# Performer attention into a top-1 mixture of experts on one core: the batch-crossing chunk on the whole PE array, and the last expert slots in another order

## The chip, the cores and the metric

The kernel runs on one core of a Trainium2 chip. The metric is the time of one execution in microseconds of device time, the median of several runs. The engines are named as the profile names them: PE (TensorE; PEld is its weight load), DVE (VectorE), ACT (ScalarE), POOL (GpSimd) and SP (SyncE, which here only issues DMAs).

## The reference

```python
# attention: B=8, H=8, S=576, D=64, m=128 features
def phi(x):
    h = einsum('bhsd,md->bhsm', x, omega) - sum(x * x, -1, keepdims=True) / 2
    return exp(h - max(h, -1, keepdims=True)) / sqrt(m)
q_p, k_p = phi(q * scale), phi(k * scale)
kv = einsum('bhsm,bhsd->bhmd', k_p, v)
z = sum(k_p, axis=2)
num = einsum('bhsm,bhmd->bhsd', q_p, kv)
den = einsum('bhsm,bhm->bhs', q_p, z)[..., None] + 1e-06
x = (num / den).transpose(0, 2, 1, 3).reshape(4608, 512)
# mixture of experts: N=4608 tokens, D=512, 8 experts, F=1024
e_idx = argmax(x @ w_gate, 1)
for e in range(8):
    mask = e_idx == e
    h = maximum(x[mask] @ w1[e], 0)
    out[mask] = gate_w[mask, None] * sigmoid(x @ w_output_gate)[mask, e, None] * (h @ w2[e])
```

## The kernel before

**Units.** The attention is cut into 32 units `u`. A unit is one head in two batches, 2 x 576 tokens, which are 9 chunks of 128 tokens. Chunks 0 to 3 lie in the first batch, chunks 5 to 8 in the second, and chunk 4 has 64 tokens of either. Every float32 operand goes to PE as a float16 high half and a float16 low half, and a product is three matmuls: high by high, high by low, low by high. For each unit the step `pn` (in `attend`) multiplies the query features `et` (the weights that are loaded) by `kvs` (the moving operand: one column for the denominator, 64 of the numerator and 16 of the two gates, so 81 a batch). A chunk needs three matmuls. `pn` is cut in two at chunk 5, so that it fits a PSUM bank; the first part has chunks 0 to 4. Since `kvs` differs between the batches, chunk 4 is done twice in halves: its first 64 tokens against the first batch, its last 64 against the second, each with half of the PE array's columns (`128*64` in the profile). The step `xf` (in `divide`) then runs on DVE: add and scale the denominator, take its reciprocal, multiply. `xf` is what the gates and the experts work on.

**Slots.** The experts work on lists of tokens, 128 a list, called slots and numbered `n`. The lists of a group of units are made on the chip as soon as its gates are known; slots 0 to 24 belong to the first three groups, slots 25 to 48 to the last, and with this data slots 0 to 37 run. The steps of a slot are: `gx` (POOL gathers the token rows), `xt` (a transposing DMA on SP), `hA` and `hB` on PE (the two halves of the hidden layer, 48 matmuls each, written to PSUM tiles `ph`), `relu` on ACT (makes `hh`, the high half) and `rest` on DVE (makes `hl`, the low half) for each of the two, `out(n, 0)` and `out(n, 1)` on PE (the second layer into the PSUM tile `po`; in the last group `out(n, 0)` is joined to `hB`), `os` on ACT (scales into the buffer that is stored), and `put` (POOL stores the rows by an indirect DMA). A slot with at most 64 tokens takes a narrower form of these steps; slots 25, 26, 36 and 37 are of this kind.

**Weights.** An expert's weights come by DMA as float32 and are cut into four quarters of each layer. `swh` on ACT writes the high half of a quarter (`w1h`, `w2h`) and `swl` on DVE the low half (`w1l`, `w2l`). Both stand in the program of every slot, inside a branch that does the work only if the slot's expert differs from the last one. With this data that is so for slots 4, 12, 21, 26, 31 and 37. Slot 36 has no new expert, so its `swh` and `swl` are branches that do no work; PE still waits for them before it uses the weights.

**Order.** All steps stand in one list of 3318 numbers, `ORDER`, which is written out in the file, and every engine's queue has its own steps in that order. A second list, `BANKS`, says which PSUM bank each tile has. The end of the program is inside a branch that is taken only if more slots are needed (here it isn't). The puts of the last slots that can run (`LATE` of them, slots 34 to 37) are issued on POOL behind that branch and a drain of POOL's DMAs; their rows wait in the buffer `xt32`.

Of the kernel before, what the change touches and what calls it, by code (L numbers as in the profile page):

```python
# [10 lines left out]
F32 = mybir.dt.float32  # L11
# [4 lines left out]
ALU = mybir.AluOpType  # L16
# [5 lines left out]
P = 128  # L22
# [5 lines left out]
NC = 9  # L28
NCV = 10
NP = H // 2  # L30
# [35 lines left out]
LATE = 4  # L66
# [258 lines left out]
def attention_moe(ctx: ExitStack, tc: tile.TileContext, kqt, kqn, v, om, wg, w1, w2, cf, cm, ci, out):  # L325
# [162 lines left out]
    kvs = buf("kvs", 2, [2, W, 2], F16)  # L488
    kvf = buf("kvf", 2, [2, P], F16)
    xf = buf("xf", 2, [NC, D + GW], F32)  # L490
    den = buf("den", 2, [NC], F32)
    xs = buf("xs", 2, [NC, P], F32)
    lga = buf("lga", 2, [NC, GW], F32)

# [1279 lines left out]
```

## Time and profile before

| | us |
|---|---|
| median of 3 runs | 628.85 (627.51 to 632.21) |
| the profiled execution | 623.89 |
| its span | 622.0 |
| PE busy | 593.9 (95%) |
| ACT busy | 421.6 (68%) |
| DVE busy | 387.9 (62%) |
| POOL busy | 374.3 (60%) |

The span is the time from the first instruction to the last in the profiled execution; 1.89 us lie around it. An engine is busy while an instruction of it runs. Matmuls are pipelined, so their durations overlap: what a matmul costs PE is the time from its start to the next one's.

### The profile page before, as it was taken

The page shows a single profiled execution, that of the slowest core. Times are in us where ns is not written, and L with a number is a line of the kernel's source. Part 1 is how long each engine was busy: PE and PEld are TensorE (multiplying, and loading weights), DVE is VectorE, ACT ScalarE, POOL GpSimd, SP SyncE. Part 2 cuts the span into 40 slices and gives each one's busy share as a digit, 9 for nine tenths or more (in the row PEclk, how much of TensorE's full clock was granted, in tenths as well). Part 3 has the DMA queues.
Part 4 walks back from the last instruction along what each step waited for, and adds up shares of the span by engine and source line. Part 5 has one row for each costly group of instructions (what it writes and reads, how often), then busy time and mean ns, then how long its engine had stood idle before and what let it go on. Part 6 is the DMA issues. An engine that isn't in the chain of part 4 may idle for free. (4 is left out here: it accounts for less than half of the span.)

```text
span 622.0 us, 22247 instructions
## 1 busy us (share of the span) xinstructions
PE 593.9 (95%) x8716; PEld 471.6 (76%) x8716; DVE 387.9 (62%) x1219; ACT 421.6 (68%) x978; POOL 374.3 (60%) x275
## 2 busy tenths in 40 slices
PE   6999987999999899999999999999999999999995
PEld 6999876867786677778877777778867867677764
DVE  4777699866678987647797865543783530351124
ACT  6999999789889688989868787871522521351143
POOL 2265589789976688999788889985322111211203
PEclk9999997899999999999999999999999999999998
DMA  7655689999999999999989998778676647742671
GB/s 269 201 163 167 201 266 210 222 238 268 290 270 249 225 252 209 289 199 230 298 223 260 231 196 200 175 180 212 203 163 215 205 80 215 203 99 55 132 284 50
DMA packets 145888, 129.00 MB, mean 207 GB/s; under 512 B 104270, under 2 KB 127440, under 8 KB 144464
## 3 DMA queue, kind: packets, MB, share of 16 engines
q1 hardware_dynamic: 139760, 107.45, 69.1%
q0 software_dynamic: 5984, 19.72, 10.3%
q8 instruction: 80, 1.31, 0.9%
q14 instruction: 64, 0.52, 0.3%
HBM read 83.86 MB, written 19.30 MB: 166 GB/s over the span
## 5 line engine op out<-in xcount | busy, mean ns | idle before, releaser
L1586 PE MATMUL ph<-xt,w1h 128*128 128x128 f16 (+1 forms) x2432 | 206.8, 218 | 0.8 <-ACTq L1510 0.4
L1586 PE MATMUL ph<-xt,w1l 128*128 128x128 f16 (+1 forms) x1216 | 203.1, 218 | 0.4 <-DVEq L1515 0.4
L1586 PEld LDWEIGHTS <-w1h 128*128 128x128 f16 x2432 | 184.3, 98 | 9.0 <-issue 1.3
L623 ACT ACTIVATE ef<-pp,nb 128x128 f32<-128x128 f32 x576 | 163.0, 394 | 17.3 <-DVE nb L617 13.1
L604 DVE TENSOR_REDUCE pp<-pp 128x3 f32<-128x384 f32 x192 | 102.8, 557 | 33.2 <-PE pp L582 28.2
L1586 PEld LDWEIGHTS <-w1l 128*128 128x128 f16 x1216 | 118.5, 98 | 0.5 <-DVEq L1515 0.5
L646 POOL TENSOR_TENSOR es<-ef,es 128x1152 f16<-128x1152 f32 x44 | 104.5, 2385 | 20.1 <-ACT es L644 13.4
L1597 DVE SCALAR_TENSOR_TENSOR hl<-ph,hh 128x512 f16<-128x512 f32 (+1 forms) x76 | 50.4, 664 | 97.8 <-ACTq L1515 61.4
L1617 PE MATMUL po<-w2h,hl 128*128 128x512 f16 x280 | 106.1, 379 | 1.8 <-DVE hl L1597 1.8
L1617 PE MATMUL po<-w2h,hh 128*128 128x512 f16 x280 | 106.2, 379 | 0.2 <-PE ph L1586 0.2
L1617 PE MATMUL po<-w2l,hh 128*128 128x512 f16 x280 | 106.1, 379 | 0.0
L1549 POOL DMA_INDIRECT gx<-rows,gi x38 | 38.2, 1005 | 104.4 <-ACT os L1672 46.1
L1593 ACT ACTIVATE hh<-ph 128x512 f16<-128x512 f32 (+1 forms) x76 | 44.6, 590 | 83.0 <-PE ph L1586 69.3
L1617 PEld LDWEIGHTS <-hh 128*128 128x128 f16 x560 | 51.3, 98 | 52.7 <-issue 0.3
L516 POOL TENSOR_TENSOR xlo<-xt,xhi 128x1152 f16<-128x1152 f32 x24 | 57.2, 2383 | 10.8 <-ACT xhi L509 8.6
L1617 PEld LDWEIGHTS <-hl 128*128 128x128 f16 x280 | 27.4, 98 | 35.4 <-DVE hl L1597 2.5
L1672 ACT ACTIVATE os<-po,gx 128x512 f32<-128x512 f32 (+1 forms) x34 | 23.4, 687 | 43.8 <-PE po L1617 37.6
L644 ACT CAST es<-ef 128x1152 f16<-128x1152 f32 x44 | 51.5, 1181 | 0.7 <-ACTq L1510 0.2
L802 PE MATMUL pn<-kvs,et 128*128 128x81 f16 (+1 forms) x960 | 47.5, 204 | 0.9 <-ACT ef L623 0.5
L802 PEld LDWEIGHTS <-et 128*128 128x128 f16 (+1 forms) x960 | 40.5, 101 | 7.6 <-issue 0.5
L582 PE MATMUL pp<-omh,xhi 64*128 64x128 f16 x432 | 42.6, 223 | 2.9 <-ACT ef L623 1.9
L582 PE MATMUL pp<-omh,xlo 64*128 64x128 f16 x432 | 41.1, 222 | 0.7 <-POOL xlo L516 0.7
(193 smaller groups left out, 1059.6 us busy)
## 6 DMA issues: line engine op xcount, KB each, us to landing
r<-w SPq DMA_DIRECT2D x10, 2048.0 KB, 9.0
xt<-kqt SPq DMA_DIRECT2D x32, 576.0 KB, 5.3
xn<-kqn SPq DMA_DIRECT2D x24, 576.0 KB, 5.7
rawv<-v SPq DMA_DIRECT2D x32, 325.0 KB, 5.4
rows<-xs SPq DMA_DIRECT2D x16, 576.0 KB, 6.0
r<-w SPq DMA_DIRECT2D x8, 512.0 KB, 6.3
ef<-w SPq DMA_DIRECT2D x2, 512.0 KB, 3.9
et<-w SPq DMA_DIRECT2D x2, 512.0 KB, 8.0
```

The lines of the kernel that those rows point to most:

```text
L516: lambda t0=t0, t1=t1: nc.gpsimd.tensor_tensor(out=xl(u)[:, t0:t1], in0=xt32(u)[:, t0:t1], in1=xh(u)[:, t0:t1], op=ALU.subtract),
L582: nc.tensor.matmul(banks["pp", 2 * u + i, g][:, c, :], x[r, t], w[r, :], start=(a == 0), stop=(a == len(ops) - 1))
L604: nc.vector.tensor_reduce(out=pp[:, 3, 0:3], in_=pp[:, 0:3, :], op=ALU.min, axis=AX.X)
L623: nc.scalar.activation(ef(n)[:, c, :], banks["pp", n, g][:, c % 3, :], AF.Exp, bias=nb(n)[:, c : c + 1], scale=-SK)
L644: nc.scalar.copy(es(slot_es(n))[:, 0], ef(n))
L646: nc.gpsimd.tensor_tensor(out=es(slot_es(n))[:, 1], in0=ef(n), in1=es(slot_es(n))[:, 0], op=ALU.subtract)
L802: nc.tensor.matmul(pn[lo:hi, c - c0, :], a[:, c, lo:hi], w[:, :, b], start=(i == 0), stop=(i == len(ops) - 1))
L1549: nc.gpsimd.indirect_dma_start(out=gx(n), out_offset=None, in_=rows[0 : (j + 1) * NC * P], in_offset=bass.IndirectOffsetOnAxis(ap=tabs[gr] ...
L1586: nc.tensor.matmul(ph[:, f4, 0:w_], w[qd][:, kk, fo : fo + P], xt(n)[:, x, 0:w_], start=(a == 0), stop=(a == 3 * KC - 1))
L1593: nc.scalar.activation(hh(n)[:, sl, 0:w_], banks["ph", n, g][:, :, 0:w_], AF.Relu)
L1597: nc.vector.scalar_tensor_tensor(out=hl(n)[:, sl, 0:w_], in0=banks["ph", n, g][:, :, 0:w_], scalar=0.0, in1=hh(n)[:, sl, 0:w_], op0=ALU.ma ...
L1617: nc.tensor.matmul(po, x(n)[:, f, :], w[f // 2][:, f % 2, :], start=(f == 0 and a == 0), stop=(f == FC - 1 and a == 2))
```

## The change

There are three edits.

1. From unit 10 on, chunk 4 is multiplied on the whole array: each of its three matmuls has 128 weight columns (all tokens of the chunk) and 162 moving columns (`kvs` of both batches side by side). The result takes two rows of the PSUM tile, which is now 6 x 81; the upper 64 lanes of the first and the lower 64 of the second are products that nobody reads. `divide` adds and inverts 6 denominators instead of 5, and a further DVE instruction multiplies the upper 64 lanes of chunk 4. Units 0 to 9 stay as they were.
2. `LATE` is 3 instead of 4: `put(34)` has its place before the branch, and its rows lie in an `os` buffer.
3. `ORDER` differs at two places: on PE, `out(24, 1)` stands ahead of `hA(25)` instead of behind it, and the steps of slots 35 to 37 on PE, DVE and ACT have another order. `BANKS` has the same numbers.

```diff
+MID = NC // 2
+ABREAST = 10
...
-LATE = 4
+LATE = 3
...
-    den = buf("den", 2, [NC], F32)
+    den = buf("den", 2, [NC + 1], F32)
...
             for c in range(c0, c1):
-                parts = [(0, P, 0 if c < 4 else 1)] if c != 4 else [(0, P // 2, 0), (P // 2, P, 1)]
+                if c == MID and abreast:
+                    for i, (a, w) in enumerate(ops):
+                        nc.tensor.matmul(
+                            pn[:, c - c0 : c - c0 + 2, :], a[:, c], w.rearrange("p w b -> p b w"), start=(i == 0), stop=(i == len(ops) - 1)
+                        )
+                    continue
+                parts = [(0, P, 0 if c < MID else 1)] if c != MID else [(0, P // 2, 0), (P // 2, P, 1)]
...
+        abreast = u >= ABREAST
+
+        def blocks(c0, c1):
+            return c1 - c0 + (abreast and c0 <= MID < c1)
 
         def divide(c0, c1):
             pn = banks["pn", u, c0]
-            dn = den(u)[:, c0:c1]
+            n = blocks(c0, c1)
+            dn = den(u)[:, c0 + (c0 > MID) :][:, 0:n]
...
             nc.vector.tensor_tensor(
-                out=xf(u)[:, c0:c1, :], in0=pn[:, :, 1:], in1=dn.unsqueeze(2).broadcast_to([P, c1 - c0, D + GW]),
+                out=xf(u)[:, c0:c1, :], in0=pn[:, 0 : c1 - c0, 1:], in1=dn[:, 0 : c1 - c0].unsqueeze(2).broadcast_to([P, c1 - c0, D + GW]),
                 op=ALU.mult,
             )
+            if n > c1 - c0:
+                nc.vector.tensor_tensor(
+                    out=xf(u)[P // 2 :, MID, :], in0=pn[P // 2 :, n - 1, 1:], in1=dn[P // 2 :, n - 1 : n].broadcast_to([P // 2, D + GW]), op=ALU.mult
+                )
...
-                tiles=[("et", u), ("kvs", u)], bank=(cls, ("pn", u, c0), [c1 - c0, W]),
+                tiles=[("et", u), ("kvs", u)], bank=(cls, ("pn", u, c0), [blocks(c0, c1), W]),
```

**PE, the end of unit 31's first `pn`** (`pn_31_0` is the PSUM tile, `et31` the query features, `w1h0` a quarter of the expert weights). Before, from the last matmul of chunk 3 on; of the six halves the first two and the last stand here:

```order
L802 MATMUL pn_31_0_10698<-kvs31_10346,et31_10441 128x81
L802 LDWEIGHTS et31_10441
L802 MATMUL pn_31_0_10698<-kvs31_10346,et31_10441 64x81
L802 LDWEIGHTS et31_10441
L802 MATMUL pn_31_0_10698<-kvs31_10346,et31_10441 64x81
...
L802 MATMUL pn_31_0_10698<-kvs31_10346,et31_10441 64x81
L1586 LDWEIGHTS w1h0_91
L1586 MATMUL ph_21_0_10717<-xt21_10439,w1h0_91 128x128
```

and now, with all three matmuls of chunk 4:

```order
L812 MATMUL pn_31_0_10656<-kvs31_10305,et31_10400 128x81
L805 LDWEIGHTS et31_10400
L805 MATMUL pn_31_0_10656<-kvs31_10305,et31_10400 128x162
L805 LDWEIGHTS et31_10400
L805 MATMUL pn_31_0_10656<-kvs31_10305,et31_10400 128x162
L805 LDWEIGHTS et31_10400
L805 MATMUL pn_31_0_10656<-kvs31_10305,et31_10400 128x162
L1605 LDWEIGHTS w1h0_91
L1605 MATMUL ph_21_0_10672<-xt21_10398,w1h0_91 128x128
```

The six matmuls of 64 lanes became three of 128 lanes and twice the columns; what stands around them is the same.

**DVE, the steps of slots 36 and 37** (`w1l1<-r1` is a quarter of slot 37's first layer, `w2l0<-r2` one of its second; rows that read `es`, `et`, `ef` or `xs` belong to slot 36 and are not run; `hl36`, `hl37` are `rest`, here in the narrow form `128x4x64`). Before, with the branches and the wide forms left out:

```order
L433 SCALAR_TENSOR_TENSOR w1l1_96<-r1_107,w1h1_92 128x1024
...
L433 SCALAR_TENSOR_TENSOR w1l0_95<-r1_107,w1h0_91 128x1024
...
L1597 SCALAR_TENSOR_TENSOR hl36_15317<-ph_36_0_15234,hh36_15295 128x4x64
...
L1597 SCALAR_TENSOR_TENSOR hl36_15317<-ph_36_1_15383,hh36_15295 128x4x64
...
L433 SCALAR_TENSOR_TENSOR w2l3_106<-xs17_11756,w2h3_102 128x1024
...
L433 SCALAR_TENSOR_TENSOR w1l2_97<-r1_107,w1h2_93 128x1024
...
L1597 SCALAR_TENSOR_TENSOR hl37_15649<-ph_37_0_15575,hh37_15629 128x4x64
...
L433 SCALAR_TENSOR_TENSOR w2l2_105<-r2_108,w2h2_101 128x1024
...
L433 SCALAR_TENSOR_TENSOR w2l3_106<-r2_108,w2h3_102 128x1024
...
L1597 SCALAR_TENSOR_TENSOR hl37_15649<-ph_37_1_15658,hh37_15629 128x4x64
```

and now:

```order
L1616 SCALAR_TENSOR_TENSOR hl36_15282<-ph_36_0_15190,hh36_15277 128x4x64
...
L437 SCALAR_TENSOR_TENSOR w1l1_96<-r1_107,w1h1_92 128x1024
...
L437 SCALAR_TENSOR_TENSOR w1l0_95<-r1_107,w1h0_91 128x1024
...
L1616 SCALAR_TENSOR_TENSOR hl36_15282<-ph_36_1_15287,hh36_15277 128x4x64
...
L437 SCALAR_TENSOR_TENSOR w1l3_98<-r1_107,w1h3_94 128x1024
...
L437 SCALAR_TENSOR_TENSOR w2l3_106<-xs17_11712,w2h3_102 128x1024
...
L437 SCALAR_TENSOR_TENSOR w2l2_105<-r2_108,w2h2_101 128x1024
...
L1616 SCALAR_TENSOR_TENSOR hl37_15614<-ph_37_0_15553,hh37_15609 128x4x64
...
L437 SCALAR_TENSOR_TENSOR w2l3_106<-r2_108,w2h3_102 128x1024
...
L1616 SCALAR_TENSOR_TENSOR hl37_15614<-ph_37_1_15621,hh37_15609 128x4x64
```

The first half of slot 36 moved ahead of the quarters of slot 37's first layer, those quarters moved ahead of the branches of slot 36's second layer, and the third quarter of slot 37's second layer moved ahead of slot 37's first `rest`.

**POOL, behind the last gather.** The change, from the gather of slot 37 on:

```order
L1568 DMA gx37_15019<-rows_69,gi3_11599 128x528
...
L1402 TENSOR_LOAD ctl3_11116
L1590 COMPARE_AND_BRANCH
L1678 DMA out0<-os34_15013,r_oi_12049 9216x256
...
L1678 DMA out0<-os34_15013,r_oi_12049 4608x512
```

Before, no put stands between that gather and the branch around the rest; the put of slot 34 stood behind the drain, ahead of those of slots 35 to 37. On PE the order of these slots is now `hB(35), hA(36), hB(36), out(35, 1), out(36, 1), hA(37), hB(37), out(37, 1)`; `out(35, 1)` stood between `hA(36)` and `hB(36)`. On ACT `relu(36, 0)`, `relu(36, 1)` and `os(36)` moved forward against slot 37's `swh`, and `relu(37, 0)` stands behind all of these.

## Rows read from the trace of the kernel before

**Rows 1.** The page's first part: busy time of each engine over the span.
```profile
PE 593.9 (95%) x8716; PEld 471.6 (76%) x8716; DVE 387.9 (62%) x1219; ACT 421.6 (68%) x978; POOL 374.3 (60%) x275
```
**Rows 2.** Timeline of PE: start, duration, tile, count, wait before it and what ended it.
```profile
208.35 0.39 PE L1617 MATMUL po<-w2h,hl 128*128 128x512 f16 x1 [1.83 <-DVE hl L1597]
...
240.25 0.27 PE L758 MATMUL kv<-cmt,kvs 128*128 128x128 f16 x2 [1.09 <-DVE nb L617]
...
260.50 0.70 PE L719 MATMUL kv<-vs,es 128*128 128x65 f16 x17 [0.63 <-POOL es L646]
```
**Rows 3.** Groups by line and shape, line 802 (count, busy us, mean ns, idle before).
```profile
L802 PE MATMUL pn<-kvs,et 128*128 128x81 f16 x768 | 39.8, 202 | 0.9 <-ACT ef L623 0.5 <-DVE xf L815 0.3
L802 PE MATMUL pn<-kvs,et 128*64 128x81 f16 x192 | 10.1, 214 | 0.0
```
**Rows 4.** Timeline of PE, the end of unit 31's first `pn`, in two stretches.
```profile
438.06 0.63 PE L802 MATMUL pn<-kvs,et 128*128 128x81 f16 x12
...
438.62 0.31 PE L802 MATMUL pn<-kvs,et 128*64 128x81 f16 x6
438.87 0.29 PE L1586 MATMUL ph<-xt,w1h 128*128 128x128 f16 x2
```
**Rows 5.** Timeline of PE, matmuls of 128 and of 512 moving columns.
```profile
583.25 0.22 PE L1586 MATMUL ph<-xt,w1l 128*128 128x128 f16 x1
583.31 0.38 PE L1617 MATMUL po<-w2h,hh 128*128 128x512 f16 x1
583.52 0.38 PE L1617 MATMUL po<-w2l,hh 128*128 128x512 f16 x1
```
**Rows 6.** Groups by line and shape, the multiplication of `divide` on DVE.
```profile
L815 DVE TENSOR_TENSOR xf<-pn,den 128x400 f32<-128x400 f32 x32 | 18.0, 566 | 0.6
L815 DVE TENSOR_TENSOR xf<-pn,den 128x320 f32<-128x320 f32 x32 | 15.5, 485 | 0.8
```
**Rows 7.** Timeline around slots 24 to 26: PE, DVE, PE.
```profile
482.93 0.38 PE L1617 MATMUL po<-w2h,hl 128*128 128x512 f16 x1
483.53 0.27 PE L1586 MATMUL ph<-xt,w1h 128*128 128x128 f16 x2 [0.23 <-DMA xt<-gx]
...
497.39 0.68 DVE L1597 SCALAR_TENSOR_TENSOR hl<-ph,hh 128x512 f16<-128x512 f32 x1
...
498.63 0.38 PE L1617 MATMUL po<-w2h,hh 128*128 128x512 f16 x1
```
**Rows 8.** Timeline of PE, the end: slots 36 and 37.
```profile
607.74 0.28 PE L1586 MATMUL ph<-xt,w1h 128*128 128x128 f16 x2
...
613.92 0.30 PE L1609 MATMUL po<-w2h,hh 128*64 128x256 f16 x2 [0.27 <-ACT hh L1593]
...
615.07 0.30 PE L1609 MATMUL po<-w2h,hl 128*64 128x256 f16 x2 [0.73 <-DVE hl L1597]
...
616.08 0.28 PE L1609 MATMUL po<-w2h,hl 128*64 128x256 f16 x2
```
**Rows 9.** Timeline of DVE, the end: slot 37's weights and `rest`.
```profile
609.63 2.35 DVE L433 SCALAR_TENSOR_TENSOR w2l<-r,w2h 128x1024 f16<-128x1024 f32 x2
...
612.32 2.36 DVE L433 SCALAR_TENSOR_TENSOR w2l<-r,w2h 128x1024 f16<-128x1024 f32 x2
614.60 0.41 DVE L1597 SCALAR_TENSOR_TENSOR hl<-ph,hh 128x256 f16<-128x256 f32 x1
```
**Rows 10.** Timeline of ACT, the end: slot 37's last quarters and `relu`.
```profile
611.23 2.00 ACT L429 ACTIVATE w2h<-r 128x1024 f16<-128x1024 f32 x2 [0.17 <-ACT hh L1593]
...
613.50 0.37 ACT L1593 ACTIVATE hh<-ph 128x256 f16<-128x256 f32 x1
```
**Rows 11.** The chain that ended last (start, us, what), and POOL's last put.
```profile
592.33 9.42 DMA gx<-rows,gi
...
603.52 5.95 POOLq L1719
...
617.17 0.97 POOL L1659 DMA_INDIRECT out<-xt,r_oi  x1 [1.64 <-ACT xt L1672]
```

More of the change, by code (lines that the diff above doesn't have):

```diff
@@ L130 @@
 ORDER = """
[134 rows of a table removed]
[135 rows of a table added]
 """
 BANKS = """
-0123456710245316527301604230675104326743061345742513406235671026457301624061570426513753124076354061371074356234703516
-7435107163465716342047657264103567415302745514726305147530267414306215063271407516204612356431547531245673461027510643
-2547130654372164507312506457236105634721406524102364736051244276503270165603257105623715027265703416720614253107646231
-5402673142675312605346175260741523640735140673251046723504167235041627350461235704612335335335335335335335335335335335
+01234567102453165273016042306751043267430613457425134062356710264573016240615704265137531240763540613710743562347035
+16743510716346571634204765726410356741530274551472630514753026741430621506327140751620461235643154753124567346102751
+06432547130654372164507312506457236105634721406524102364736051244276503270165603257105623715027265703416720614253107
+64623154026731426753126053461752607415236407351406732510467235041672350416273504612357046123353353353353353353353353
+35335335
 """
```

269 rows, old and new, of the table ORDER are left out of this document.

## The prediction

> **What bounds the kernel now.** I read the busy times first, then what PE waits for, then the end. PE is busy for 593.9 us of a span of 622.0, and no other engine for more than 421.6 [rows 1]. So time that is taken off PE's stream is taken off the whole, wherever PE isn't about to wait for somebody else anyway. After unit 10 has begun PE's only long waits until the end are the three of [rows 2]: 1.83 us for DVE's low half of a hidden layer, 1.09 us for a bias that DVE writes, 0.63 us for POOL. What PE saves in the unit that leads up to such a wait lengthens the wait. The end is another matter: there the last slot's weights are being cut by ACT and DVE while PE waits for them, 0.27 and 0.73 us in the last two microseconds of matmuls [rows 8]. The last put follows these [rows 11].
>
> **Chunk 4 on the whole array: PE.** In [rows 4] the last matmuls of unit 31's first part are in view. Twelve whole ones begin at 438.06; the group lasts 0.63 us and one of them 0.202 [rows 3], so they start 0.428/11 = 0.039 us apart, and the next thing could start at 438.06 + 12 x 0.039 = 438.53. It starts at 438.87, so the six halves cost 0.34 us. They begin only at 438.62, 0.09 later than a whole one would, and the last of them starts about 438.62 + 0.31 - 0.214 = 438.72, 0.15 us ahead of the next matmul of full width. So there is a gap on both sides, and between them the halves run about 0.02 us apart, much closer than whole matmuls do: the halves of the two sides overlap, and what they save in that way the two gaps take back.
>
> The Trainium skill bears on both sides of this. Its page "TensorEngine Tiling (Array Packing)" says under Key Properties that changing the tiling mode drains the engine, which agrees with a gap on either side of the halves in [rows 4]. "TensorE: Matmul & The Clock Gate" says in the table of "Why this matters for your kernels" that matmuls of fewer than 128 output rows run concurrently when each has a column group of its own, which speaks against this change, and agrees with their 0.02 us spacing; if only this rule counted, the case would be the last rival below.
>
> The new form has three matmuls of 162 columns, a shape that the trace doesn't have. A matmul of 512 columns takes 583.52 - 583.31 = 0.21 us, one of 128 columns 0.06 [rows 5]. By columns that is 0.066 from the first and 0.076 from the second; 128 is the nearer, so I take 0.076, 0.23 for three, and no gap, since the form stays that of the matmuls around it. The saving is 0.34 - 0.23 = 0.11 us a unit, by the other row 0.14. Units 10 to 31 are 22: 2.4 us, at most 3.1. Three weight loads go away with the three matmuls; PE's loads overlap its matmuls, so I count nothing for them. What of it reaches the end: four units lie right ahead of the waits of [rows 2] or share one with them, and theirs is lost, 4 x 0.11 = 0.45.
>
> **Chunk 4 on the whole array: DVE.** `divide` gets one more instruction a unit, 64 lanes by 80 elements. The multiplications of 400 and 320 elements take 566 and 485 ns [rows 6], so 80 elements cost 81 ns and an instruction without any elements 485 - 4 x 81 = 161. One of 80 elements then lies between 0.08 us (when all that is fixed overlaps its neighbours) and 0.24; I take 0.15, since small instructions that follow each other on DVE overlap in part. That is 3.3 us of DVE in 22 units, bounds 1.8 and 5.3, beside PE's stream on an engine that is busy for 62% of the span. It is queued ahead of DVE's next work (the minima of the next unit, `rest`), and its readers on POOL and PE get `xf` that much later. Where PE has work of the slots queued it is hidden by that; where the chain to one of the three waits runs through DVE, it is not: four such units, 0.08 to 0.24 each, I take 0.4 in all. The reciprocal and the addition have 6 columns instead of 5, a few nanoseconds that I leave out. **Chunk 4 then gives 2.4 - 0.45 - 0.4 = 1.55 us**; by the ends, 3.1 - 0.3 = 2.8 and 2.4 - 0.45 - 5.3 = -3.3.
>
> **Slots 24 and 25.** Before, PE begins `hA(25)` when the transposed rows of slot 25 have landed: its last matmul of `out(24, 0)` starts at 482.93 and the next one at 483.53, where 0.21 would do [rows 7, 5]. So 0.39 us are lost. With `out(24, 1)` between, twelve matmuls or 2.6 us, the rows have landed long before. Against it, `hA(25)` ends 2.2 us later, and with it the first `relu` of slot 25 on ACT, behind which ACT's cutting of slot 26's weights is queued. The next place where PE can feel that is slot 26's second layer at 498.63, whose `rest` is done at 497.39 + 0.68 = 498.07 [rows 7]: 0.56 us to spare against an ACT that comes perhaps as much later. I count a gain of 0.3, bounds -0.3 and 0.4.
>
> **The end.** Before, DVE is the one that ends last: from 609.63 on it works without a wait through two quarters, slot 37's first `rest`, two more quarters (612.32, 2.36 us) and the second `rest` (614.60 to 615.01) [rows 9], and PE's matmul that reads it starts at 615.07 after a wait of 0.73 [rows 8]. In the new order slot 37's first layer is cut earlier on DVE, while PE still has `hB(36)` and the two second layers; the branches of slot 36 cost PE 0.2 to 0.5 us wherever an engine reaches them late, and I leave `hA(37)` at its 607.74 [rows 8]: what `hB(36)` gains by being pulled ahead, slot 36's second layer loses, since its branches on DVE now stand behind two quarters more. ACT makes slot 37's last two quarters ahead of `relu(37, 0)`: two quarters take 2.00 us [rows 10], done at about 611.7, the two `relu` (0.37 each) at 612.2 and 612.7. DVE then has the first `rest` (0.41) to 612.6, one quarter (1.18) to 613.8 and the second `rest` to 614.25, against 615.01. PE starts `out(37, 0)` at 612.6, 0.7 us later than now, and is through with it at 614.1, as the `rest` is done; twelve pairs 0.11 apart (as 615.07 to 616.08 has nine) start the last at about 615.3 instead of 616.08. `os` and the put follow as before. I take 0.85, bounds -0.7 (ACT's longer chain ahead of `relu(37, 0)` late by as much as one quarter and a half `relu` more) and 1.6 (both waits of [rows 8] gone and half of the weights' branches with them).
>
> `put(34)` moves ahead of the branch on POOL. Its rows are behind the gather of slot 37 in POOL's DMA queue, which takes from 592.33 to 601.75 [rows 11], so it lands at perhaps 602.4, and the drain that ran from 603.52 for 5.95 us finds it done. The puts behind the drain are three instead of four, but the last one waits for `os(37)` either way (1.64 us of wait at 617.17). I count nothing; if the drain is later by the put's landing, the last put could start 1 us late.
>
> **Sum.** 1.55 + 0.3 + 0.85 = 2.7 us. Against the profiled execution, 623.89 - 2.7 = 621.2; that execution lies 4.96 us below the median of 628.85, so the median becomes 628.85 - 2.7 = **626.15**. A measurement of this kernel can tell about 1%, 6.3 us, from no change: the forecast is well inside it.
>
> **Rivals.**
> DVE's extra instruction is on the path more often: if half of the 22 units feel it, 11 x 0.15 = 1.65 are lost instead of 0.4, and the sum is 1.45: 627.4. For it: PE waits for DVE in two of three places of [rows 2]. Against it: DVE has 38% of its time free. Chance 0.12.
> The end gives nothing, because the drain or ACT's longer chain takes what DVE gives: 1.85 are left, 627.0. For it: POOL's chain to the last put has 1.64 us of air only [rows 11]. Chance 0.10.
> Slower: the two gaps belong to the change of chunk, not to the half form, and stay, while the overlap of the halves is given up. Six halves then cost 0.34 - 0.22 of gaps = 0.12 and the new three 0.23: 0.11 more a unit, 2.4 us in 22, and DVE's 0.4 on top; with 0.3 and 0.85 from the slots the time is 628.85 + 1.65 = 630.5. It decides from the point where the gaps that stay are over 0.11 us a unit. For it: the trace can't show the new shape. Against it: twelve whole matmuls of four chunks follow each other 0.039 apart with no gap. Chance 0.05.
>
> **Chances and range.** The forecast has 0.70; 0.03 are left for what I don't see. The range: chunk 4 at 2.8, the slots at 0.4 and the end at 1.6 make 624.05; the milder rivals make 627.4; the slower one 630.5. The runs of the kernel before lie 1.3 below and 3.4 above their own median, and a part of that is in any median of three, so I go 0.75 below the one and 2.6 above the other: 623.3 to 630.0, which leaves the slower rival out. By 1%: faster (under 622.6) 0.06, within 0.91, slower (over 635.1) 0.03.
>
> **What would show it.** Right: no `128*64` at `pn` after unit 9; the matmul behind the first `pn` of unit 31 starts 0.70 us after its first whole one instead of 0.81; an extra multiplication of 64 x 80 with a start-to-start near 0.15; PE without the 0.23 wait at slot 25; the last second-layer matmul 0.8 us nearer to the end of PE's earlier work. Wrong, if the 162-column matmuls are more than 0.11 apart, if new waits of PE for `xf`, `nb` or `hl` appear in units 10 to 31, or if `relu(37, 0)` comes later than 613. It would be wrong as a whole if the waits of [rows 2] grew by what PE saves in many more units than four.

## The result, and the profile after

The changed kernel is slower: 633.37 us against 627.88 (medians of 20 runs each), a ratio of 1.0077 with a 95% interval of 1.0056 to 1.0098, about 4.8 us. The ratio leaves out executions over 1.5% above the fastest of their kernel, so it isn't the quotient of the two medians. The forecast was 626.15, faster by 2.7. The profiled execution of the changed kernel has a span of 634.9 us, 12.9 more than that of before. Much of this isn't the change: its time of 636.69 lies 3.3 above its own median, and that of before, 623.89, lies 4 below the median of before.

The page's first part, as in [rows 1]:

```profile
PE 594.9 (94%) x8650; PEld 471.8 (74%) x8650; DVE 393.8 (62%) x1241; ACT 422.3 (67%) x978; POOL 374.5 (59%) x275
```

PE has 66 matmuls less and DVE 22 instructions more, as the diff says. PE's busy time is no lower, and what it stands idle has grown from 28.1 to 40.0 us. In unit 31 the chunk does what was forecast. PE's timeline at the end of its first `pn`, as in [rows 4], from two stretches:

```profile
444.85 0.63 PE L812 MATMUL pn<-kvs,et 128*128 128x81 f16 x12
...
445.32 0.39 PE L805 MATMUL pn<-kvs,et 128*128 128x162 f16 x3
445.55 0.27 PE L1605 MATMUL ph<-xt,w1h 128*128 128x128 f16 x2
```

The next work starts 0.70 us after the first matmul, where it was 0.81 [rows 4]. The three wide matmuls take 445.55 - 445.32 = 0.23 us, and there is no gap on either side of them: 0.11 us are saved. But this isn't so in every unit. In unit 25 the next work on PE is `pp`, the projection of a later unit onto its features, whose matmuls use 64 of the array's rows (`64*128`). Before and after:

```profile
351.63 0.87 PE L802 MATMUL pn<-kvs,et 128*128 128x81 f16 x18
352.44 0.23 PE L582 MATMUL pp<-omh,xhi 64*128 64x128 f16 x2
```

```profile
357.04 0.63 PE L812 MATMUL pn<-kvs,et 128*128 128x81 f16 x12
357.50 0.39 PE L805 MATMUL pn<-kvs,et 128*128 128x162 f16 x3
357.82 0.23 PE L586 MATMUL pp<-omh,xhi 64*128 64x128 f16 x2
```

Here the three wide matmuls take 357.82 - 357.50 = 0.32 us, 0.09 more than in unit 31, and the next work starts 0.78 us after the first matmul, where it was 0.81. The gap on the far side stays where the next matmul has another form. So it is in 9 of the 22 units (12, 13, 16, 18, 21, 24, 25, 26 and 28), in both traces of the changed kernel. Added up over the 22 units by the matmuls' starts, as the forecast did for unit 31, chunk 4 costs 7.4 us before and 5.9 after: PE saves 1.5 us, not 2.4.

DVE's groups by line and shape, as in [rows 6], with the added multiplication last:

```profile
L830 DVE TENSOR_TENSOR xf<-pn,den 128x400 f32<-128x400 f32 x32 | 18.2, 567 | 0.6
L830 DVE TENSOR_TENSOR xf<-pn,den 128x320 f32<-128x320 f32 x32 | 15.5, 485 | 0.8
...
L835 DVE TENSOR_TENSOR xf<-pn,den 64x80 f32<-64x80 f32 x22 | 5.4, 244 | 0.8
```

The added one lasts 0.244 us, the upper bound of the forecast. But it costs more than it lasts. DVE's timeline in a unit late in the attention, before and after:

```profile
394.02 0.56 DVE L815 TENSOR_TENSOR xf<-pn,den 128x400 f32<-128x400 f32 x1
394.50 0.68 DVE L1597 SCALAR_TENSOR_TENSOR hl<-ph,hh 128x512 f16<-128x512 f32 x1
395.10 0.56 DVE L604 TENSOR_REDUCE pp<-pp 128x3 f32<-128x384 f32 x1
...
396.23 0.20 DVE L769 SCALAR_TENSOR_TENSOR kvs<-kv,kvs 128x32 f16<-128x32 f32 x1 [0.18 <-DVEq L1510]
```

```profile
399.51 0.56 DVE L830 TENSOR_TENSOR xf<-pn,den 128x400 f32<-128x400 f32 x1
400.11 0.24 DVE L835 TENSOR_TENSOR xf<-pn,den 64x80 f32<-64x80 f32 x1
400.38 0.69 DVE L1616 SCALAR_TENSOR_TENSOR hl<-ph,hh 128x512 f16<-128x512 f32 x1
...
402.12 0.20 DVE L773 SCALAR_TENSOR_TENSOR kvs<-kv,kvs 128x32 f16<-128x32 f32 x1 [0.17 <-DVEq L1529]
```

From the start of the multiplication to the next work it is 394.50 - 394.02 = 0.48 us before and 400.38 - 399.51 = 0.87 after: 0.39 more. The instruction that followed before began 0.08 us before the multiplication ended; the added one begins 0.04 us after it has ended, and the next 0.03 after that. In 17 of the 22 units the difference is 0.37 to 0.40 us; in the other five DVE waits for something else at that place, before or after. The added instruction works on lanes 64 to 127 alone, its neighbours from lane 0 on; whether that is what holds it and the next one back, no run tests. `kvs` (the next unit's moving operand for `pn`) is late by just this: from the start of the multiplication it takes 402.12 - 399.51 = 2.61 us instead of 2.21. PE, which needs it in the next `pn`, stands (PE's timeline, after):

```profile
401.73 0.20 PE L812 MATMUL pn<-kvs,et 128*128 128x81 f16 x1
402.37 0.39 PE L812 MATMUL pn<-kvs,et 128*128 128x81 f16 x6 [0.44 <-DVE kvs L773]
```

Before, PE doesn't wait there (its `pn` starts at 396.25 with no wait).

### The profile page after: what moved, and what is told of

It reads as the page before. It is cut to its first block, busy times and chain, and to the rows that moved or that the text cites. A ratio compares the mean times of both kernels' runs of the same rounds, so it can differ in the third digit from the quotient of the medians.

```text
span 634.9 us, 22139 instructions
## 1 busy us (share of the span) xinstructions
PE 594.9 (94%) x8650; PEld 471.8 (74%) x8650; DVE 393.8 (62%) x1241; ACT 422.3 (67%) x978; POOL 374.5 (59%) x275
## 5 line engine op out<-in xcount | busy, mean ns | idle before, releaser
L1605 PE MATMUL ph<-xt,w1h 128*128 128x128 f16 (+1 forms) x2432 | 208.9, 219 | 9.4 <-issue 4.0
L812 PE MATMUL pn<-kvs,et 128*128 128x81 f16 (+1 forms) x828 | 43.2, 205 | 2.9 <-DVE nb L621 0.8
L812 PEld LDWEIGHTS <-et 128*128 128x128 f16 (+1 forms) x828 | 37.2, 100 | 8.4 <-issue 2.5
L586 PEld LDWEIGHTS <-xhi 64*128 64x128 f16 x864 | 32.9, 95 | 12.5 <-issue 4.8
```

The costliest lines, as they stand in the source:

```text
L586: nc.tensor.matmul(banks["pp", 2 * u + i, g][:, c, :], x[r, t], w[r, :], start=(a == 0), stop=(a == len(ops) - 1))
L812: nc.tensor.matmul(pn[lo:hi, c - c0, :], a[:, c, lo:hi], w[:, :, b], start=(i == 0), stop=(i == len(ops) - 1))
L1605: nc.tensor.matmul(ph[:, f4, 0:w_], w[qd][:, kk, fo : fo + P], xt(n)[:, x, 0:w_], start=(a == 0), stop=(a == 3 * KC - 1))
```

## The experiments

Two theories stood at first: S, that the swap of slots 24 and 25 carries the loss (in the trace after, PE is 2.9 us later at the end of `hB(26)`, against the changed kernel's own delay ahead of the swap), and U, that the first edit does. The later ones were D, that within the first edit it is DVE's further multiplication, and F, that it is the place of PE's instructions, which are 132 fewer by unit 31. The kernels of a batch ran on one chip, beside the kernel before. The first batch took the change apart.

`pn_only`, the first edit alone: the changed kernel with `ORDER` as before, and

```diff
-LATE = 3
+LATE = 4
```

> Only the first edit: chunk 4 on the whole array from unit 10 on, the order and the late puts as before. If the swap of slots 24 and 25 carries the loss (theory S), this kernel is 1 to 2 us faster than the kernel before, as the prediction had it. If the extra DVE instruction and the shifted transposing DMAs of the units carry it (theory U), it is 3 to 5 us slower.

`swap_only`, on the kernel before (positions 2593 and 2594 of `ORDER`, cut from their line):

```diff
-2618 2642 2619 2652
+2618 2619 2642 2652
```

> Only out(24, 1) ahead of hA(25). Theory S: slot 26's weights overwrite the quarters that hA(25) still reads, so ACT and DVE begin them 2.2 us later and PE waits for them in hB(25), hA(26) and hB(26): 2.5 to 3 us slower. Theory U: within 0.5 us of the kernel before, the 0.56 us to spare hold.

`tail_only`, on the kernel before (and the new order of positions 2921 to 2966):

```diff
-LATE = 4
+LATE = 3
```

> Only the order of slots 35 to 37 and the put of slot 34 ahead of the branch. Both theories: 0.8 to 1.5 us faster. If it is slower, the end is a third source of the loss.

`no_swap`, on the changed kernel (cut from the line likewise):

```diff
-2618 2619 2642 2652
+2618 2642 2619 2652
```

> The changed kernel with slots 24 and 25 in the order of before. Theory S: 3 us faster than the changed kernel and 2 to 3 us faster than the kernel before. Theory U: still 3 us slower than the kernel before.

| against the kernel before, 628.55 us | median, us | ratio | 95% interval |
|---|---|---|---|
| pn_only | 636.41 | 1.0129 | 1.0083 to 1.0174 |
| swap_only | 628.63 | 0.9994 | 0.9962 to 1.0026 |
| tail_only | 628.82 | 1.0017 | 0.9988 to 1.0046 |
| no_swap | 633.88 | 1.0056 | 1.0022 to 1.0090 |

S falls: the swap alone changes nothing, and without it the changed kernel is still slower. The loss is the first edit's; `pn_only` lost more than was expected of it, and `tail_only` did not gain. The 2.9 us at slot 26 in the trace after were not the swap's: what stands there in PE's timeline of `swap_only` is one wait of 0.70, in place of the 0.23 of [rows 7],

```profile
494.73 0.20 PE L1587 MATMUL ph<-xt,w1l 128*128 128x64 f16 x1 [0.70 <-DVEq L1516]
```

while the changed kernel has this wait too and two more further on, which nothing releases (PE's timeline, after):

```profile
502.16 0.23 PE L1605 MATMUL ph<-xt,w1l 128*128 128x128 f16 x1 [0.56 <-issue]
506.34 0.22 PE L1605 MATMUL ph<-xt,w1h 128*128 128x128 f16 x1 [1.52 <-issue]
```

(Slot 26 runs in the wide form, as these rows show; it is not of the narrow kind that the section on the kernel before counts it to.) Such idle times without a releaser, inside a step, led to theory F. The second batch took the first edit apart.

`pn_no_mult`, on pn_only:

```diff
-            if n > c1 - c0:
-                nc.vector.tensor_tensor(
-                    out=xf(u)[P // 2 :, MID, :], in0=pn[P // 2 :, n - 1, 1:], in1=dn[P // 2 :, n - 1 : n].broadcast_to([P // 2, D + GW]), op=ALU.mult
-                )
```

> The first edit without its further multiplication: the upper 64 lanes of chunk 4 are not divided in units 10 to 31, so their tokens are wrong; PE's stream is that of pn_only. If the loss of pn_only comes from DVE's extra instruction (theory D), this kernel is 2 us faster than the kernel before. If it comes from PE's own stream, which is 132 instructions shorter by unit 31 so that its instruction loads fall at other places and some of them late (theory F), it is 4 to 8 us slower, with idle time that no semaphore ends at the places of pn_only.

`dve_only`, on the kernel before:

```diff
+            if u >= 10 and c0 <= NC // 2 < c1:
+                nc.vector.tensor_tensor(
+                    out=xf(u)[P // 2 :, NC // 2, :], in0=pn[P // 2 :, NC // 2 - c0, 1:],
+                    in1=dn[P // 2 :, NC // 2 - c0 : NC // 2 - c0 + 1].broadcast_to([P // 2, D + GW]), op=ALU.mult
+                )
```

> The kernel before with one further multiplication of 64 lanes by 80 in units 10 to 31 (the upper half of chunk 4 a second time, the same values); PE is unchanged. Theory D: 4 to 8 us slower. Theory F: at most 1 to 2 us slower, and no idle time at the places of pn_only.

`pn_pad`, on pn_only:

```diff
                 if c == MID and abreast:
+                    for i, (a, w) in enumerate(ops):
+                        nc.tensor.matmul(pn[:, c - c0, 0:1], a[:, c], w[:, 0:1, 0], start=True, stop=True)
```

> pn_only with three matmuls of one column ahead of chunk 4's, in the same units, into a column that is overwritten: PE has as many instructions again as before, and the matmuls cost it at most 3 x 0.04 us a unit, about what the whole array saves. Theory F: the idle times at the places of pn_only go, and the kernel is within 2 us of the kernel before. Theory D: as slow as pn_only, plus up to 2 us.

| against the kernel before, 624.35 us | median, us | ratio | 95% interval |
|---|---|---|---|
| pn_no_mult | 653.74 | 1.0463 | 1.0423 to 1.0502 |
| dve_only | 627.23 | 1.0043 | 1.0010 to 1.0075 |
| pn_pad | 626.53 | 1.0032 | 1.0001 to 1.0063 |

The time of `pn_no_mult` tells nothing of either theory: 29 us are more than either could give. Undivided rows go into the gates, tokens go to other experts, and the slots have other work: its page counts 24 `w1h` quarters of the usual kind where the others have 20, so one more expert's weights were loaded. Its trace departs from the others only at 430 us, by a wait of 12.9 us; up to there it shows what PE does without the multiplication. PE's waits at three places, from the traces of this batch and of the fourth:

| PE's wait, us | before | pn_no_mult | dve_only | pn_third | pn_pad2 |
|---|---|---|---|---|---|
| `pp` at about 146, for a branch on DVE | none shown | 0.23 | 0.51 | 0.51 | 0.51 |
| `kv` at about 241, for `nb` | 1.09 | 0.81 | 1.47 | 1.49 | 1.51 |
| `pn` at about 397, for `kvs` | none shown | none shown | 0.44 | 0.44 | 0.44 |

The second row in `pn_no_mult` and in `dve_only`:

```profile
241.49 0.27 PE L762 MATMUL kv<-cmt,kvs 128*128 128x128 f16 x2 [0.81 <-DVE nb L621]
```

```profile
240.69 0.27 PE L758 MATMUL kv<-cmt,kvs 128*128 128x128 f16 x2 [1.47 <-DVE nb L617]
```

By the starts of the same matmuls PE falls back against the trace of before at eight places from 145 to 411 us, mostly by 0.2 to 0.6 us each: 2.6 us together in `dve_only`, 2.6 in `pn_third`, 2.6 in `pn_pad2`, and nothing (-0.1) in `pn_no_mult`. So these are the multiplication's. A part comes back at later waits that PE has anyway. `dve_only`, with a time 2.7 us above that of before, agrees with theory D; `pn_pad` agrees with F, unless this batch was kinder: its kernel before is 4 us faster than that of the first.

The third batch tested the placement with no work added. The wide form of slot 25's `hB` is jumped over with this data, so matmuls put there are not run and only shift what follows. `pn_again` is pn_only; `pn_skip` and `after_skip` are pn_only and the changed kernel with 66 such pairs, `before_skip` the kernel before with 62:

```diff
         def hidden_and_second(w_):
+            if n == 25 and w_ == P:
+                for _ in range(66):
+                    nc.tensor.matmul(banks["ph", n, 1][:, 0, 0:1], w1h[2][:, 0, 0:P], xt(n)[:, 0, 0:1], start=True, stop=True)
             hidden(1, w_)
```

> pn_only once more, on the same chip as the next three. 3 to 8 us slower than the kernel before, with idle PE in the slots at the three places of pn_only: in slot 26's first hidden half and twice further on.

> pn_only, and 66 matmuls with their weight loads in the wide form of slot 25's hB, which is jumped over with this data. Nothing more is executed, but from there on PE's instructions lie where they lay in the kernel before. Theory F (instruction loads that come late, by their place in PE's stream): the idle times in the slots go, and it is 3 to 5 us faster than pn_only; 1 to 3 us over the kernel before are left from DVE's instruction and the units. Theory D: as slow as pn_only.

> The kernel before with 62 such pairs in the same form that is jumped over: PE's instructions of the later slots then lie as in pn_only, modulo 16 KB, and nothing else is changed. Theory F: 3 to 5 us slower than the kernel before, with idle PE at the places of pn_only. Theory D: no change.

> The changed kernel with the 66 pairs in the form that is jumped over. Theory F: 2 to 5 us faster than the changed kernel, so within 2 us of the kernel before. Theory D: no change against the changed kernel, 4 to 6 us slower than before.

| against the kernel before, 629.10 us | median, us | ratio | 95% interval |
|---|---|---|---|
| pn_again | 633.67 | 1.0071 | 1.0045 to 1.0097 |
| pn_skip | 634.71 | 1.0082 | 1.0050 to 1.0115 |
| before_skip | 630.35 | 1.0017 | 0.9989 to 1.0045 |
| after_skip | 633.12 | 1.0054 | 1.0022 to 1.0086 |

By the times F fails here: restoring the places gave nothing back to `pn_skip`, and `before_skip` lost 1.1 us where 3 to 5 were expected (`after_skip` had no changed kernel beside it). By the traces it is right about the idle times. PE's timeline of `before_skip`, in the middle of a hidden half, at a matmul where the kernel before runs on:

```profile
546.30 0.22 PE L1586 MATMUL ph<-xt,w1l 128*128 128x128 f16 x1
548.22 0.28 PE L1586 MATMUL ph<-xt,w1h 128*128 128x128 f16 x2 [1.69 <-issue]
```

This is the same matmul of the program as the one below in `pn_third`, and as those in pn_only, pn_again, no_swap and the changed kernel, which stand idle there for 1.1 to 1.7 us (in pn_only and no_swap the profile names a branch on ACT); in `pn_skip` and `after_skip` PE doesn't stop there. Instead `pn_skip` has a new stop behind the lengthened jump, at the start of slot 26:

```profile
500.36 0.40 PE L1605 MATMUL ph<-xt,w1h 128*128 128x128 f16 x2 [3.40 <-issue]
```

So the cure had a price of its own (2.24 us at the same matmul in `after_skip`), and the test of the time isn't clean. Nor do the times pay all that a trace shows: the profiled execution of `before_skip` took 634.96 us, 4.6 above its median.

The fourth batch put pn_only (`pn_third`), `pn_pad2` (pn_pad), `dve_only2` (dve_only) and `after_pad` (the changed kernel with pn_pad's lines) on one chip.

> pn_only a third time, on the same chip as pn_pad2 and dve_only2, since pn_only and pn_pad ran in different calls, whose kernels before differ by 4 us. 4 to 8 us slower than the kernel before.

> pn_pad again. If PE's instruction places carry a share of their own, it is at least 2 us faster than pn_third on the same chip and has no idle PE at its places; if the difference between the calls was the chip alone, the two are within 1 us.

> dve_only again: 2 to 3.5 us slower than the kernel before, with PE's waits where chunk 4's further multiplication stands in the chain, whatever the chip. If it is within 1 us of it, DVE's share was the other chip's.

> The changed kernel with the three one-column matmuls a unit of pn_pad. If the shares add up, 1 to 3 us slower than the kernel before, where the changed kernel is 4.8 us slower; if the swap or the end adds to it, 4 to 5 us.

| against the kernel before, 625.17 us | median, us | ratio | 95% interval |
|---|---|---|---|
| pn_third | 628.60 | 1.0035 | 1.0005 to 1.0065 |
| pn_pad2 | 626.81 | 1.0035 | 0.9999 to 1.0071 |
| dve_only2 | 626.61 | 1.0005 | 0.9979 to 1.0031 |
| after_pad | 626.23 | 1.0004 | 0.9978 to 1.0029 |

PE's timeline of `pn_third` at that matmul:

```profile
544.11 0.22 PE L1605 MATMUL ph<-xt,w1l 128*128 128x128 f16 x1
546.23 0.28 PE L1605 MATMUL ph<-xt,w1h 128*128 128x128 f16 x2 [1.91 <-issue]
```

Shortly before, a packet of the DMA queue that the page calls instruction (q8, one packet of 16 KB about every 8 us) has landed, at 544.81. The DMA view of the stretch from 543.6 to 544.9 has it, that from 544.9 to 546.3 has none:

```profile
q8 instruction: 1, 0.02, 5.5%
```

In the seven traces that stop at this matmul the packet landed 1.3 to 1.5 us before PE goes on; in the others (`pn_no_mult`, whose slots differ, aside) it had landed 3.4 us or more before, and PE runs on. The kernels with 132 PE instructions less have 79 such packets, those with as many as before 80. Of the 22 stops of 0.9 us or more without a releaser, in all traces behind the first 60 us, 21 end 1.2 to 1.9 us behind the landing of such a packet. So the stops go with late loads of PE's instructions.

`pn_pad2` does not stop there, yet the two have the same ratio. It has more to do on PE: with the three small matmuls chunk 4 costs 7.5 us in the 22 units by the same sum, against 6.0 in `pn_third`, so that about 1.5 us must have come back elsewhere. `dve_only2` and `after_pad` were expected 2 to 3.5 and 1 to 3 us slower than the kernel before, and are 0.3. The fifth batch, at last, had the changed kernel (`after_again`), its padded form (`after_pad2`) and `dve_only3` on one chip.

> The changed kernel once more, so that it stands beside its padded form on one chip. 3 to 6 us slower than the kernel before.

> after_pad again. If the places of PE's instructions carry most of the loss, within 1 us of the kernel before and 3 us or more faster than after_again. If they carry little and DVE's multiplication the most, within 1 us of after_again.

> dve_only a third time: 0.3 us and 2.7 us slower so far. If DVE's multiplication carries most of the loss, half or more of what after_again loses; else within 1.5 us of the kernel before.

| against the kernel before, 628.82 us | median, us | ratio | 95% interval |
|---|---|---|---|
| after_again | 633.40 | 1.0104 | 1.0050 to 1.0158 |
| after_pad2 | 633.32 | 1.0063 | 1.0028 to 1.0098 |
| dve_only3 | 633.31 | 1.0086 | 1.0051 to 1.0122 |

Here DVE's multiplication alone, with PE, the order and the puts as before, loses nearly as much as the whole change, which also saves 1.5 us on PE. PE stands in `dve_only3` at the place shown above for the changed kernel, with the same number:

```profile
400.85 0.20 PE L802 MATMUL pn<-kvs,et 128*128 128x81 f16 x1
401.49 0.58 PE L802 MATMUL pn<-kvs,et 128*128 128x81 f16 x11 [0.44 <-DVE kvs L769]
```

No version beat the kernel before.

## Why the prediction was wrong, step by step

**PE's part was right in form and too large.** Where the work behind chunk 4 is of full width, 0.11 us a unit are saved and there are no gaps around the wide matmuls: the row after has 0.70 where the forecast had 0.70. The forecast took this for all 22 units, from one row. In the 9 units where the 64-row `pp` follows, the far gap stays and about 0.01 us is saved, so the term of 2.4 us measures 1.5. The rival in which the gaps stay and the time grows is out: no unit's chunk 4 became dearer. The list of PE's long waits was short by one, too, right behind unit 10's `pn` (PE's timeline, before):

```profile
133.63 0.21 PE L582 MATMUL pp<-omh,xhi 64*128 64x128 f16 x1 [1.16 <-ACT ef L623]
```

**DVE's part was mis-sized, and this is the step that failed.** The forecast took 0.15 us for the instruction, bounds 0.08 and 0.24, and let 0.4 us of it reach the end, in four units. It bounded the price by durations and assumed that the instruction overlaps its neighbours. It overlaps neither: 0.39 us from start to start, 22 x 0.39 = 8.6 us of DVE instead of 3.3, where DVE has no other wait. And "DVE has 38% of its time free" was the wrong view to cover it with: DVE's place in the chain counts, not its share. The instruction stands between `pn` and the next unit's `nb` and `kvs`, for which PE waits a moment later, so it opened waits where there had been none (0.44 at `kvs`) and lengthened others (1.09 to 1.47 at `nb`): eight places and 2.6 us in the traces, none of them in `pn_no_mult`. The rival "DVE's extra instruction is on the path more often" had the mechanism, with a chance of 0.12 and 1.65 us lost; `dve_only` lost 0.3, 2.7 and 5.4 us (0.0005 x 625, 0.0043 x 624 and 0.0086 x 629). That is up to more than the 1.5 us of PE, and the sign turns.

**A term that the sum didn't have.** The forecast counted nothing for PE's stream being 132 instructions shorter. In the traces this moves stops of 1 to 2 us into the slots (1.63, 1.52 and 1.91 in `pn_third`, 5.1 us together, which its time doesn't show in full).

**Slots 24 and 25.** Forecast a gain of 0.3 with bounds -0.3 and 0.4; `swap_only` gives 0.9994, 0.4 us faster, with 2.4 faster and 1.6 slower inside the interval. The wait for the transposed rows went, as forecast, and slot 25's second hidden half now waits 0.70 for the branches on DVE that stand behind slot 26's weights: nothing is left of it in the trace.

**The end.** Forecast a gain of 0.85, bounds -0.7 and 1.6; `tail_only` gives 1.0017, which leaves room for 0.8 us of gain and 2.9 of loss. `relu(37, 0)`, which was to come by 613, comes at 615.24 in `tail_only`. The working had left out one wait. `os(35)` stands on ACT ahead of slot 37's second-layer quarters, and `out(35, 1)`, which it needs, had moved behind `hB(36)`. ACT's timeline of `tail_only`:

```profile
610.50 0.69 ACT L1673 ACTIVATE xt<-po,gx 128x512 f32<-128x512 f32 x1 [2.57 <-PE po L1618]
611.09 1.99 ACT L430 ACTIVATE w2h<-r 128x1024 f16<-128x1024 f32 x2
```

Before, these quarters were under way as soon as ACT had the first layer, with `os(35)` long done. Part of `out(35, 1)`'s lateness is again an idle time that nothing releases, in the middle of that step; `after_pad`, `after_pad2` and `after_skip` have it too, with 1.6 to 2.0 us (PE's timeline of `tail_only`):

```profile
606.24 0.38 PE L1618 MATMUL po<-w2h,hl 128*128 128x512 f16 x1
608.35 0.39 PE L1618 MATMUL po<-w2h,hh 128*128 128x512 f16 x1 [1.74 <-issue]
```

The drain and `put(34)` took nothing that the runs show.

**The sum.** The first edit lost 2.2 to 8.1 us instead of gaining 1.55 (pn_third 0.0035 x 625, pn_only 0.0129 x 629), the other two gave nothing instead of 1.15.

**What stays open.** How much of the first edit's loss belongs to the places of PE's instructions. That their shift moves stops of 1 to 2 us to the same matmuls in kernels that share the placement, and that these stops follow late instruction packets, is shown in the traces; what makes a packet late is not. In the times the padded kernels are level with the plain ones (1.0035 and 1.0035) or 0.0041 lower with intervals that overlap (1.0063 against 1.0104), which is 0 to 2.6 us; with the 1.5 us that they do more on PE, an estimate of the places' share is 1.5 to 4.1 us. By another estimate, the plain kernels save 1.5 us on PE that `dve_only` doesn't, and yet lose 1.9 us more (1.0035 against 1.0005) or 1.1 more (1.0104 against 1.0086): 2.6 to 3.4 us. The intervals are as wide as these shares.

Why DVE's instruction costs 0.3 to 2.7 us in the batches whose kernel before takes 624 to 625 us and 5.4 in one that takes 629 is open too; the first edit shows the same split (1.0035 against 1.0071 and 1.0129). The traces have a mark of it: PE's wait of 1.83 us at 208 [rows 2] is in all of the second and fourth batch, the faster ones, and in none of the others. It is in the one trace of before, whose time of 623.89 belongs to these, and not in the trace after. So the two traces that were compared first are not of one kind: `swap_only` and `tail_only`, whose times are those of before, have spans of 628.4 and 626.3 us against its 622.0. It isn't the chip by number: the record has chip 4 for the second batch and for the fifth.

## What to carry to other kernels

Price an added instruction by start to start between neighbours that depend on it in the same way, not by its duration, and then look at what stands behind it in its engine's queue and who waits for that: an engine that is busy for 62% can be the one that others wait for, and 0.39 us there cost up to more than 0.11 us saved on the engine that is busy for 95%. Read a saving per unit in several units before it is multiplied: 9 of 22 had another neighbour and saved next to nothing. Where several edits come together, run each alone: two of the three here were neutral, and the trace of the whole put 2.9 us at the place of one of them. One profiled execution can hold idle times that the median doesn't pay for, so a loss that is read from a trace needs a kernel that has this loss alone. A run whose time is spoilt can still hold the answer in its trace, up to where its work departs.

## What the hardware showed that was not expected

- A DVE multiplication of lanes 64 to 127 by 80 that follows one of 128 lanes by 400 on the same tiles lasted 0.244 us and cost 0.39: it began 0.04 us after the other had ended, where the usual next instruction begins 0.08 before (0.60 against 0.48 from start to start).
- Three matmuls of 128 lanes by 162 columns took 0.23 us in front of work of full width (unit 31) and 0.32 in front of matmuls on 64 of the array's rows (unit 25).
- PE stopped for 0.9 to 3.4 us where no semaphore was waited for, and 21 of 22 such stops ended 1.2 to 1.9 us behind the landing of a 16 KB packet of the instruction queue.
- 62 matmuls with their weight loads that are never run, put into a branch that is jumped over, made PE stop at three later matmuls (1.20 and 1.25 us in slot 26, 1.69 us at 548) where the kernel before runs on; with 66 of them, in `pn_skip`, there was one stop of 3.40 us behind the jump.
- DVE's instruction alone cost 0.9% in one batch (1.0086) and 0.05% in another (1.0005).
